# An adaLN block on one core: the first piece of w_mod is issued by ScalarE instead of SyncE

## The chip, the cores and the metric

The kernel runs on one core of one Trainium2 chip. Five engines work side by side, each through its own list of instructions: TensorE (PE: matmuls; PEld: the loading of their stationary operand), VectorE (DVE), ScalarE (ACT), GpSimd (POOL) and SyncE (SP). SP and ACT also issue DMA transfers, each on a queue of its own; the transfers of both queues are carried out by the core's 16 DMA engines. The metric is the time of one execution in microseconds (us).

## The reference

The block takes x, 2048 rows of 640 numbers, and a conditioning vector c of 640.

```
mod = silu(c) @ w_mod          # 640 x 3840: six vectors sa, ca, ga, sb, cb, gb of 640 each
h = layernorm(x) * (1 + ca) + sa
x = x + ga * (attention(h @ wqkv) @ wo)      # 32 heads of 20, causal, window of 256
h = layernorm(x) * (1 + cb) + sb
x = x + gb * ((sigmoid(h @ w_gate) * (h @ w_up)) @ w_down)     # 1536 hidden
```

Everything is stored in bfloat16. What matters here is the first line and the first layernorm: before the first projection with wqkv can run, sa and ca must be known. They come from silu(c) and the first 1280 columns of w_mod.

## The kernel before, in words

The rows of x are worked through in 8 chunks of 256 rows (two blocks of 128). For each chunk the kernel normalises, projects to q, k and v, computes windowed attention, projects with wo, normalises again and runs the MLP. The work of neighbouring chunks is interleaved.

The order is written out by hand. Each operation is registered by `Prog.op` (alias `A`) in the order of the code, and gets its place from the table `PRIO`: the number divided by 5 is its place, and the remainder says which engine runs it, in the order of `ENGS` (0 PE, 1 ACT, 2 DVE, 3 POOL, 4 SP). `schedule` goes through the operations in the order of these numbers, appends each to its engine's list, gives each DMA the next one of 24 semaphores in turn, and gives each tile a buffer. `emit` writes the five lists with their semaphore waits. Within an engine the order is fixed: an instruction whose operand has not come holds all behind it.

The head of the kernel, up to the first projection, is as follows.

- Loads, all through the helper `dma` (its issues carry line 570 in the profile). ACT issues c (1.2 KB, into a corner of the tile oT), then x block 1 (160 KB). SP issues x block 0 (160 KB), then the first 1280 columns of w_mod in five pieces of 128 rows each (`load_bulk` with the tag wm0; 320 KB each, into wd, which is free until the MLP's weights come), then pieces of wqkv with further blocks of x between them. ACT has no other DMA in the head; after its two issues it loads the table for tanh.
- PE first runs matmuls on zeros (line 649, `warm`), three operations of two matmuls each. Then it turns c into a column (line 634), adds a matmul of ones to the accumulator of the modulation, and runs two more operations of `warm`. Then come the five groups of the modulation, one for each piece of w_mod (`fnA`; through line 668, like all matmuls made by `mm`), with a filling matmul on zeros (line 660, `fill`) between them. The ten transposes of the normalised x blocks 0 and 1 stand between the fourth and the fifth group.
- DVE computes the statistics of x block 0 (line 776, two instructions), then c_col, siluc and silubc (the silu of c, repeated 64 times as a matmul operand; lines 636, 638, 640; ACT computes the tanh in it, line 637), then the statistics of x block 1. GpSimd computes the power of minus one half (lines 781 and 783), and DVE normalises both blocks (line 796).
- The transposes are copied out of PSUM into hT (line 839), and once the five groups are through, DVE copies sa and 1 + ca out (mA, line 761). ACT and DVE modulate hT (lines 846 and 847), and the first projection starts (line 668, operands wqkv and hT).

The lines that issue the loads of the head:

```
keep[0], keep[1] = load_x(p_x1, 0, 0), load_x(p_x1, 1, 0, eng="act", tmin=1.25)
load_bulk(wm_ap[0], wm_src[:, :, 0:1280], Rm[0], 0.93, 0.2, "wm0", lat=0.9)
for i in range(4):
    load_w3(320 * i, 320 * i + 320, 1.1, 0.30 + 0.005 * i, "wq" if i < 2 else "wk", lat=0.5)
```

Of the kernel before, what the change touches and what calls it, by code (L numbers as in the profile page):

```python
# [22 lines left out]
SM_SCALE = 1.0 / math.sqrt(DH)  # L23
VW = 22
NDMA = 24
SWITCH = 0.095
ENGATTR = {"pe": "tensor", "act": "scalar", "dve": "vector", "pool": "gpsimd", "sp": "sync"}
ENGS = ("pe", "act", "dve", "pool", "sp")
OVERLAP = {"pe": 0.0, "act": 0.085, "dve": 0.075, "pool": 0.045, "sp": 0.0}


class Res:
# [49 lines left out]
class Prog:  # L82
# [69 lines left out]
    def schedule(self):  # L152


        free = {e: START for e in ENGS}
        bw = 0.0
        lastturn = False
# [4 lines left out]
        pemode = 0  # L162
        portend = 0.0
        freed = {}

        def slot_time(pool, s):
            ten = pool.tenant[s]
            if ten is None:
                if not all(x.done for x in pool.init[s]):
                    return None  # L170
                return max([x.end + x.lat for x in pool.init[s]], default=0.0)
            return None if ten.left else freed[ten]

        def take(t, s):
            ten = t.pool.tenant[s]
            t.prev = list(t.pool.init[s]) if ten is None else list(ten.rel)
            t.slot = s
            t.pool.tenant[s] = t

        for o in sorted(self.ops, key=lambda x: x.prio):  # L180
            assert all(d.done for d in o.deps), o.tag
            e = ENGS[o.prio % 5]
            assert e in o.engs, (o.tag, e)
            o.eng = e
            st = max([o.tmin, free[e] + (SWITCH if e == "pe" and o.mode != pemode else 0.0)]
                     + [d.end + (0.0 if d.eng == "pe" and e == "pe" else d.lat) for d in o.deps])
            if o.isdma and e == "sp":
                st = max(st, bw - QMAX)
            for t in o.tiles:
                if t.slot is None:  # L190
                    step = 1 if t.mate is None else 2
                    best = None
                    for s in range(0, len(t.pool.tenant), step):
                        rts = [slot_time(t.pool, s + k) for k in range(step)]
                        if None not in rts and (best is None or max(rts) < best[0]):
                            best = (max(rts), s)
                    assert best is not None, (o.tag, t.name)
                    if t.mate is None:
                        take(t, best[1])
                    else:  # L200
                        take(t, best[1] + t.odd)
                        take(t.mate, best[1] + 1 - t.odd)
                for x in t.prev:
                    st = max(st, x.end + x.lat)
            if e == "dve" and o.port:
                st = max(st, free["pool"])
            elif e == "pool":
                st = max(st, portend)
            o.start = st
            if e == "pe":  # L210
                pemode = o.mout
            dur = o.dur[e]
            free[e] = st + dur - OVERLAP[e]
            if e == "dve" and o.port:
                portend = free[e]
            if o.isdma:
                turn = o.dlat > 3.0
                if e == "sp" and bw - st > 2.0:
                    free[e] += 0.35 if o.dur[e] > 1.0 else 0.1
                bw = max(st + o.dlat, bw + (MIXED if turn != lastturn and bw > st + o.dlat else 0.0)) + o.work  # L220
                lastturn = turn
                o.end = max(bw - 0.83, st + dur)
                s = rr
                rr = (rr + 1) % NDMA
                dmacnt[s] += 16
                o.key, o.val = f"d{s}", dmacnt[s]
                if dmalast[s] is not None:
                    o.deps.append(dmalast[s])
                dmalast[s] = o
            else:  # L230
                o.end = st + dur
            order[e].append(o)
            o.done = True
            for t in o.tiles:
                t.left -= 1
                if t.left == 0:
                    last = {}
                    for x in t.ops:
                        if x.isdma:
                            last[x] = x  # L240
                    for e2 in ENGS:
                        xs = [x for x in t.ops if x.eng == e2 and not x.isdma]
                        if xs:
                            last[e2] = max(xs, key=lambda x: x.start)
                    t.rel = list(last.values())
                    freed[t] = max(x.end + x.lat for x in t.rel)
        self.order = order
        self.span = max(o.end for o in self.ops)

    def emit(self):  # L250
        nc = self.nc
# [85 lines left out]
def c_pe(n):  # L337
    return max(n, 64) / 2400.0 + 0.0027


PE_EPS = 0.14
PRIO = [
# [117 lines left out]
]  # L460
TR1 = 2
NPH = 3
NPQ = 2
PQ = ()
KEEP = 3
DSAFE = 1.5
START = 0.8
PORTLAG = 0.05
MIXED = 0.55
NPB = 0  # L470
GB = ()
XT0 = 1
# [9 lines left out]
DEDGE = 0.245  # L482
FILL = 1
WSE = (("dve", "pool"), ("dve", "pool"))
QMAX = 4.5
WDT = 72.0
PAIR = 0
PAIRO = 0
# [5 lines left out]
def build(nc, A_x, A_wqkv, A_wo, B_x, B_w_gate, B_w_up, B_w_down, c, w_mod, out, S=2048):  # L494
# [60 lines left out]
    def R(name):  # L555
        return Res(name)
# [8 lines left out]
    def dma(dst, src, work, reads=(), writes=(), prio=50.0, tmin=0.0, tag="dma", extra=(), nonc=False, hold=(), eng="sp", lat=0.08 + DSAFE, dur=0.5, dlat=2.24):  # L565
        def fn(e, _):
            if nonc:
                with nc.allow_non_contiguous_dma(reason="small"):
                    return e.dma_start(dst(), src())
            return e.dma_start(dst(), src())  # L570
        return A(eng, fn, dur, reads=reads, writes=writes, prio=prio, work=work, tmin=tmin, tag=tag, extra=extra, hold=hold, lat=lat, dlat=dlat)
# [23 lines left out]
    def load_x(pool, b, prio, tmin=0.0, eng="sp", extra=()):  # L595
# [6 lines left out]
    wm_src = w_mod.rearrange("(t p) f -> p t f", p=128)  # L602
    Rm = [[R(f"wm{i}_{kt}") for kt in range(NDT)] for i in range(4)]
    wm23 = hhall[:, 0:2 * NDT * D].rearrange("p (t f) -> p t f", t=NDT)
    wm_ap = [wd[:].rearrange("p a b -> p (a b)")[:, 0:6400].rearrange("p (t f) -> p t f", t=NDT),
             wu[:].rearrange("p a b -> p (a b)")[:, 0:6400].rearrange("p (t f) -> p t f", t=NDT),
             wm23[:, :, D:2 * D], wm23[:, :, 0:D]]

    def load_bulk(dst, src, Rs, work, prio, tag, extra=(), cuts=(1, 2, 3, 4, 5), **kw):
        k = 0  # L610
        for m in cuts:
            dma(lambda k=k, m=m: dst[:, k:m, :], lambda k=k, m=m: src[:, k:m, :], work * (m - k), writes=Rs[k:m],
                prio=prio + 0.01 * k, tag=tag, extra=list(extra), **kw)
            k = m
# [37 lines left out]
    for i in range(5):  # L652
        o = A("pe", warm, 0.85 if i < 4 else 0.43, prio=90, reads=[R_z], extra=wprev, tag="warm", writes=[R("w")])
# [302 lines left out]
    last = {"s": fills, "p": []}  # L956
# [350 lines left out]
```

## Time and profile before

| | |
|---|---|
| Time, median of 3 runs | 325.69 us (325.58 to 326.39) |
| Span of the profiled execution, first to last instruction | 324.3 us |
| The profiled execution's own time | given by its span alone; the median of the runs is 1.39 us above it |
| PE busy | 317.3 us, 98% of the span |
| ACT, DVE, POOL busy | 212.3, 211.8, 187.2 us |
| Moved by DMA | 37.85 MB |

Lines of a timeline read: start in us from the first instruction, duration, engine, line, operation, what it writes and reads with shapes, the count of merged instructions, and in brackets the idle time of the engine just before, with what ended it. A q behind an engine's name stands for its sequencer: "ACTq DMA_DIRECT2D" is the issue of a transfer by ScalarE, not the transfer. Lines of waits read: engine, line, who was waited for, total in us, times, longest. Lines of windows read: the stretch, its length, busy time and instructions of PE, PEld, DVE, ACT and POOL, the granted clock, the DMA engines' busy share, and GB/s. Lines of DMA queues read: packets, MB, share of the 16 engines' time; q1 carries what SP issues and q10 what ACT issues. Ends of matmuls are modelled, so a busy PE is not one at its peak, and the granted clock stands at 1.00 in all windows.

### The profile page before, as it was taken

The page shows a single profiled execution, that of the slowest core. Times are in us where ns is not written, and L with a number is a line of the kernel's source. Part 1 is how long each engine was busy: PE and PEld are TensorE (multiplying, and loading weights), DVE is VectorE, ACT ScalarE, POOL GpSimd, SP SyncE. Part 2 cuts the span into 40 slices and gives each one's busy share as a digit, 9 for nine tenths or more (in the row PEclk, how much of TensorE's full clock was granted, in tenths as well). Part 3 has the DMA queues.
Part 4 walks back from the last instruction along what each step waited for, and adds up shares of the span by engine and source line. Part 5 has one row for each costly group of instructions (what it writes and reads, how often), then busy time and mean ns, then how long its engine had stood idle before and what let it go on. Part 6 is the DMA issues. An engine that isn't in the chain of part 4 may idle for free.

```text
span 324.3 us, 11594 instructions
## 1 busy us (share of the span) xinstructions
PE 317.3 (98%) x4872; PEld 222.7 (69%) x4873; DVE 211.8 (65%) x424; ACT 212.3 (65%) x316; POOL 187.2 (58%) x276
## 2 busy tenths in 40 slices
PE   8999999989999999999999999999999999999997
PEld 3564545446776568765776467877786788787885
DVE  5797898778687959674477475837463769264332
ACT  1899985889876687788687867786767764011120
POOL 5128869976668694847585939382939691012100
DMA  7998799989891383824405394340213032202101
GB/s 249 371 333 299 165 269 180 200 137 183 260 164 22 83 109 77 152 61 101 85 22 82 97 103 110 92 69 5 81 40 88 3 79 53 76 20 64 40 2 40
DMA packets 71694, 37.85 MB, mean 117 GB/s; under 512 B 45274, under 2 KB 70362, under 8 KB 71642
## 3 DMA queue, kind: packets, MB, share of 16 engines
q1 hardware_dynamic: 69616, 35.31, 48.3%
q10 hardware_dynamic: 2026, 1.80, 2.1%
q8 instruction: 38, 0.62, 0.8%
q14 instruction: 14, 0.11, 0.1%
HBM read 21.30 MB, written 5.25 MB: 82 GB/s over the span
## 4 chain that ended last, share of the span: by engine, by line
PE 73%; DMA 2%; SPq 2%; DVE 1%; POOL 1%; issue 0%; DVEq 0%
PE M L668 61%; PE S L669 6%; PE M L669 5%; DMA gbc<-gate 2%; SPq L803 2%; DVE wd L1192 1%; POOL x L793 0%; POOL st L788 0%; DVE hh L1211 0%; POOL E L1040 0%; DVE x L1230 0%; DVEq L310 0%
## 5 line engine op out<-in xcount | busy, mean ns | idle before, releaser
L1040 POOL TENSOR_SCALAR_AFFINE_SELECT E<-E 128x512 bf16<-128x512 bf16 (+1 forms) x176 | 142.6, 836 | 68.7 <-ACT E L1015 67.0
L1015 ACT ACTIVATE E<-S 128x512 bf16<-128x512 f32 (+2 forms) x184 | 150.9, 878 | 47.4 <-PE S L669 46.5
L668 PE MATMUL M<-wqkv,hT 128*128 128x480 bf16 (+1 forms) x340 | 73.9, 355 | 0.6 <-ACT hT L846 0.5
L668 PE MATMUL M<-h2T,wu 128*128 128x256 bf16 x480 | 68.0, 273 | 0.5 <-DVE hh L1211 0.5
L668 PE MATMUL M<-h2T,wg 128*128 128x256 bf16 x480 | 67.8, 273 | 0.0
L668 PE MATMUL M<-wd,hh 128*128 128x320 bf16 (+2 forms) x396 | 58.1, 295 | 0.0
L1209 ACT ACTIVATE sig<-M 128x512 f32<-128x512 f32 x48 | 28.9, 602 | 44.1 <-PE M L668 41.7
L1211 DVE SCALAR_TENSOR_TENSOR hh<-sig,M 128x512 bf16<-128x512 f32 x48 | 32.4, 681 | 37.1 <-ACT sig L1209 24.0
L668 PEld LDWEIGHTS M<-h2T,wu 128*128 128x128 bf16 x480 | 45.9, 98 | 8.4 <-issue 1.2
L668 PEld LDWEIGHTS M<-h2T,wg 128*128 128x128 bf16 x480 | 45.7, 98 | 7.1
L668 PEld LDWEIGHTS M<-wqkv,hT 128*128 128x128 bf16 x340 | 30.1, 98 | 27.6 <-DMA wqkv<-in_A_wqkv_dram 1.6
L668 PEld LDWEIGHTS M<-wd,hh 128*128 128x128 bf16 x396 | 36.8, 98 | 14.3 <-DVE hh L1211 0.2
L669 PEld LDWEIGHTS S<-QT,KT 20*64 20x64 bf16 (+1 forms) x1856 | 19.9, 100 | 21.3 <-ACT E L1015 12.0
L1230 DVE TENSOR_TENSOR x<-M,x 128x320 bf16<-128x320 f32 (+2 forms) x33 | 15.6, 476 | 27.2 <-PE M L668 27.2
L669 PE MATMUL S<-QT,KT 20*64 20x256 bf16 (+5 forms) x1856 | 32.1, 228 | 1.2 <-ACT E L1015 1.2
L776 DVE BATCH_NORM_STATS2 st<-x 128x6 f32<-128x320 bf16 x64 | 28.6, 477 | 2.3 <-DMA x<-in_A_x_dram 1.9
L1082 DVE STREAM_TRANSPOSE T<-M 128x512 f32<-128x512 f32 x32 | 21.5, 698 | 9.2 <-PE S L669 8.0
L668 PE MATMUL M<-wo,oT 128*128 128x320 bf16 x160 | 25.4, 299 | 0.0
L669 PE MATMUL M<-E,V 128*32 128x128 bf16 (+1 forms) x960 | 22.8, 246 | 0.8 <-ACT E L1015 0.4
L781 POOL TENSOR_SCALAR st<-st 128x2 f32<-128x2 f32 x16 | 3.7, 234 | 33.8 <-DVE st L778 33.6
L669 PEld LDWEIGHTS M<-E,V 128*32 128x32 bf16 x960 | 19.2, 97 | 5.3 <-issue 2.9
L1091 DVE STREAM_TRANSPOSE On<-Tn 128x1024 bf16<-128x1024 bf16 x16 | 19.8, 1240 | 0.3
(77 smaller groups left out, 240.2 us busy)
## 6 DMA issues: line engine op xcount, KB each, us to landing
x<-in_A_x_dram SPq DMA_DIRECT2D x23, 160.0 KB, 2.3
doc<-On SPq DMA_DIRECT2D x56, 40.0 KB
wd<-in_B_w_down_dram SPq DMA_DIRECT2D x4, 480.0 KB
wd<-in_w_mod_dram SPq DMA_DIRECT2D x5, 320.0 KB
wqkv<-in_A_wqkv_dram SPq DMA_DIRECT2D x4, 400.0 KB
wu<-in_w_mod_dram SPq DMA_DIRECT2D x5, 320.0 KB
oT<-doc SPq DMA_DIRECT2D x8, 192.0 KB, 2.5
out_dram<-x SPq DMA_DIRECT2D x9, 160.0 KB
```

Source lines behind the costliest of these rows:

```text
L668: return e.matmul(o, l, r, start=st, stop=sp, skip_group_check=True)
L669: return e.matmul(o, l, r, start=st, stop=sp, tile_position=tp, skip_group_check=True)
L776: A("dve", lambda e, g, bi=bi, j=j: e.bn_stats(v(bi * 12 + j * 6, 6), src[bi].ap[:, j * 320:(j + 1) * 320]), 0.48, reads=[src[bi].r()], wr ...
L781: A("pool", lambda e, g: e.tensor_scalar(v(28, n), var(), EPS, None, op0=ALU.add), 0.2, reads=[st.r(("m", bi)) for bi in range(n)], writes ...
L803: return e.dma_start_transpose(dst(), src())
L1015: A("act", lambda e, eng: e.activation(dst(), src(), ACT.Exp, scale=SM_SCALE), c_act(n), reads=[Sp.r()], writes=[E.r(key)], prio=3, tag=f" ...
L1040: A("pool", lambda e, eng: e.affine_select(rows(dst), rows(src), pattern=[[0, 8], [sign, n]], compare_op=ALU.is_ge, fill=0.0, base=base, c ...
L1082: A("dve", lambda e, g, h=h: e.transpose(T1.ap[:, 512 * h:512 * h + 512], X[h].ap), 0.694, reads=[X[h].r()], writes=[T1.r(h)], prio=3.5, t ...
L1091: A("dve", lambda e, g: e.transpose(On.ap[:], Tn.ap[:]), 1.22, reads=[Tn.r()], writes=[On.r()], prio=4, tag=f"tr2_{a}")
L1209: A("act", lambda e, g, pg=pg, sg=sg: e.activation(sg.ap[:], pg.ap[:], ACT.Tanh, scale=0.5), c_act(512), reads=[pg.r()], writes=[sg.r()], ...
L1211: A("dve", lambda e, g, pu=pu, sg=sg, f0=f0: e.scalar_tensor_tensor(out=hh.ap[:, f0:f0 + 2, :], in0=sg.ap[:].rearrange("p (a b) -> p a b", ...
L1230: A("dve", lambda e, g, ps=ps, bi=bi, c0=c0, n=n: e.tensor_tensor(x1[bi].ap[:, c0:c0 + n], ps.ap[:, 0:n], x1[bi].ap[:, c0:c0 + n], op=ALU. ...
```

## The change

The load of the first w_mod piece may now be issued by ACT or SP, and the table gives it to ACT, at place 15, where c stood. c (76 to 81), x block 0 (84 to 89) and two statistics instructions of DVE (87 to 92 and 92 to 97) move back by one place each, which changes nothing on SP and DVE: x block 0 is still SP's first issue, and the other four pieces follow it. ACT's list now begins with the first piece of w_mod, c, x block 1.

The rest of the diff takes the planner's estimate of times out of `schedule`. It had chosen each tile's buffer by these estimates; the choices are now written out in the table `SLOTS`, one number for each of 709 tiles, and they are the buffers that the estimate chose before. The first four DMA semaphores are dealt out in the new order.

```diff
 PRIO = [
-    23, 28, 258, 8, 43, 33, 958, 18, 1448, 38, 3, 507, 513, 72, 67, 48, 53, 58, 76, 84, 101, 99, 144, 149, 154, 159,
+    23, 28, 258, 8, 43, 33, 958, 18, 1448, 38, 3, 507, 513, 72, 67, 48, 53, 58, 81, 89, 101, 76, 144, 149, 154, 159,
...
-    92, 87, 187, 237, 242, 247, 253, 263, 272, 267, 280, 275, 290, 300, 305, 286, 317, 296, 322, 311, 376, 357, 386,
+    97, 92, 187, 237, 242, 247, 253, 263, 272, 267, 280, 275, 290, 300, 305, 286, 317, 296, 322, 311, 376, 357, 386,
...
             for t in o.tiles:
                 if t.slot is None:
...
+                    s = SLOTS[tiles[t]] if SLOTS else 0
+                    ten = t.pool.tenant[s]
...
-    load_bulk(wm_ap[0], wm_src[:, :, 0:1280], Rm[0], 0.93, 0.2, "wm0", lat=0.9)
+    load_bulk(wm_ap[0], wm_src[:, :, 0:1280], Rm[0], 0.93, 0.2, "wm0", lat=0.9, eng=("act", "sp"))
```

More of the change, by code (lines that the diff above doesn't have):

```diff
@@ L161, in schedule, with number @@
         rr = 0
[L162 to L178, printed above, removed]
+        tiles = {}
+        def number(t):
+            if t is not None and t not in tiles:
+                tiles[t] = len(tiles)
+                number(t.mate)
+        for o in self.ops:
+            for t in o.tiles:
+                number(t)
         for o in sorted(self.ops, key=lambda x: x.prio):
@@ L184, in schedule @@
             o.eng = e
[L185 to L188, printed above, removed]
             for t in o.tiles:
                 if t.slot is None:
[L191 to L215, printed above, removed]
-            if o.isdma:
[L217 to L223, printed above, removed]
-                rr = (rr + 1) % NDMA
[L225 to L231, printed above, removed]
+                    s = SLOTS[tiles[t]] if SLOTS else 0
@@ new lines, in schedule @@
+                    ten = t.pool.tenant[s]
+                    assert ten is not None or all(x.done for x in t.pool.init[s]), (o.tag, t.name)
+                    assert ten is None or ten.left == 0, (o.tag, t.name)
+                    t.prev = list(t.pool.init[s]) if ten is None else list(ten.rel)
+                    t.slot = s
+                    t.pool.tenant[s] = t
+            if o.isdma:
+                dmacnt[rr] += 16
+                o.key, o.val = f"d{rr}", dmacnt[rr]
+                if dmalast[rr] is not None:
+                    o.deps.append(dmalast[rr])
+                dmalast[rr] = o
+                rr = (rr + 1) % NDMA
@@ L237, in schedule @@
                     last = {}
[L238 to L244, printed above, removed]
+                    for x in sorted(t.ops, key=lambda x: x.prio):
+                        last[x if x.isdma else x.eng] = x
                     t.rel = list(last.values())
-                    freed[t] = max(x.end + x.lat for x in t.rel)
         self.order = order
-        self.span = max(o.end for o in self.ops)
     def emit(self):
@@ L460 @@
 ]
+SLOTS = [
[20 rows of a table added]
+]
 TR1 = 2
@@ L466 @@
 DSAFE = 1.5
-START = 0.8
-PORTLAG = 0.05
-MIXED = 0.55
 NPB = 0
```

7 lines of the change are left out of this document (removed), and 20 rows, old and new, of the table SLOTS.

## The prediction, made before the result was known

> **What bounds the kernel now.** I read four views in this order: the page, the whole-run waits of TensorE, the timelines of the first 16 us, and the DMA rates of that stretch. The page first:
>
> ```profile
> span 324.3 us, 11594 instructions
> ...
> PE 317.3 (98%) x4872; PEld 222.7 (69%) x4873; DVE 211.8 (65%) x424; ACT 212.3 (65%) x316; POOL 187.2 (58%) x276
> ...
> PE 73%; DMA 2%; SPq 2%; DVE 1%; POOL 1%; issue 0%; DVEq 0%
> ```
>
> TensorE is busy for 317.3 of 324.3 us, so what is left to gain or lose is the idle time of PE, and any stretch in which PE runs late. Of TensorE's waits over the whole run, these bear on the sum:
>
> ```profile
> PE S L669 <- ACT E L1015: 1.2, 4, 0.4
> PE M L668 <- DVE hh L1211: 0.5, 1, 0.5
> PE M L668 <- ACT hT L846: 0.5, 1, 0.5
> ```
>
> The first two lie in the attention and in the first MLP. The third is the end of the head: the first projection waits for the modulated hT. Because PE has almost no idle time behind it, a head that ends later pushes nearly everything behind it by the same amount. So the change is priced at the first projection. How PE gets there (PE's timeline):
>
> ```profile
> 3.98 0.18 PE L634 MATMUL M<-ident,oT 5*128 5x5 bf16 x1
> ...
> 6.04 0.58 PE L668 MATMUL S<-silubc,wd 128*128 128x64 bf16 x10
> ...
> 8.11 0.47 PE L668 MATMUL S<-silubc,wd 128*128 128x64 bf16 x10 [0.19 <-DMA wd<-in_w_mod_dram]
> 8.44 0.62 PE L668 MATMUL M<-ident,x 128*128 128x128 bf16 x8
> ...
> 10.36 2.33 PE L668 MATMUL M<-wqkv,hT 128*128 128x320 bf16 x15 [0.47 <-ACT hT L846]
> ```
>
> At 3.98 PE turns the conditioning vector c (it lands in oT), right behind the warm-up matmuls. From 6.04 it multiplies the five w_mod pieces (wd), at 8.44 it transposes the normalised x blocks 0 and 1, and at 10.36 projects. VectorE's timeline of the same time:
>
> ```profile
> 3.08 0.89 DVE L776 BATCH_NORM_STATS2 st<-x 128x6 f32<-128x320 bf16 x2 [1.42 <-DMA x<-in_A_x_dram]
> 4.20 0.17 DVE L636 TENSOR_SCALAR c_col<-M 128x5 bf16<-128x5 f32 x1 [0.23 <-PE M L634]
> ...
> 4.84 0.49 DVE L640 COPY silubc<-siluc 128x320 bf16<-128x320 bf16 x1
> 5.24 0.88 DVE L776 BATCH_NORM_STATS2 st<-x 128x6 f32<-128x320 bf16 x2
> ...
> 7.58 0.80 DVE L796 TENSOR_SCALAR x<-x,st 128x640 bf16<-128x640 bf16 x2 [1.22 <-POOL st L783]
> ...
> 9.50 0.17 DVE L761 COPY mA<-S 128x10 f32<-128x10 f32 x1
> ```
>
> This is the chain that sets the head: c_col, the copy silubc, then with no gap the statistics of x block 1 (5.24 to 6.12), the power on GpSimd, the normalisation until 8.38, and PE's transposes 0.06 us later, at 8.44. It starts from PE's 3.98. That instant is set by the warm-up in front of it, and the change does not touch it. The modulation mA follows at 9.50, behind the transposes and PE's last w_mod group.
>
> **The change part by part.** It moves one 320 KB load, the first w_mod piece, from SP's list, second place, to ACT's list, first place. The issues as they stand (timelines of ScalarE and SyncE):
>
> ```profile
> 0.79 0.57 ACTq L570 DMA_DIRECT2D oT<-in_c_dram  x1
> 1.40 0.37 ACTq L570 DMA_DIRECT2D x<-in_A_x_dram  x1
> 1.80 1.28 ACT L637 ACT_TABLE_LOAD   x1 [1.80 <-issue]
> 4.40 0.21 ACT L637 ACTIVATE cth<-c_col 128x5 f32<-128x5 bf16 x1 [1.32 <-DVE c_col L636]
> ```
> ```profile
> 0.79 0.39 SPq L570 DMA_DIRECT2D x<-in_A_x_dram  x1
> 1.25 2.31 SPq L570 DMA_DIRECT2D wd<-in_w_mod_dram  x5
> ```
>
> One w_mod issue costs 2.31 / 5 = 0.46 us of its queue. (1) On SP the four other pieces and everything behind them go out up to 0.46 us earlier. (2) The moved piece goes out at 0.79 instead of 1.25, also 0.46 earlier. (3) On ACT, c goes from 0.79 to 1.25, x block 1 from 1.40 to 1.86, the table load from 1.80 to 2.26, ending 3.54. The tanh that needs the table runs at 4.40, so the table load costs nothing: 0.86 us of idle time hide it, and past that ACT would delay silubc one for one. No wait is added and no other instruction moves.
>
> What the earlier pieces are worth: the windows of 0.5 and 1 us (last two columns: DMA share, GB/s) and the loads of weights by TensorE.
>
> ```profile
> 2.50:3.00 0.50, 0.50 (x3) 0.16 (x2) 0.00 (x0) 0.50 (x1) 0.50 (x7) 1.00 0.98 218
> 3.00:3.50 0.50, 0.50 (x3) 0.14 (x1) 0.42 (x2) 0.08 (x1) 0.50 (x3) 1.00 0.67 248
> ...
> 4.00:5.00 1.00, 1.00 (x5) 0.51 (x5) 0.60 (x4) 0.21 (x1) 0.45 (x1) 1.00 1.01 357
> ```
> ```profile
> 7.23 0.35 PEld L668 LDWEIGHTS S<-silubc,wd 128*128 128x128 bf16 x10 [0.20 <-DMA wd<-in_w_mod_dram]
> ...
> 8.10 0.35 PEld L668 LDWEIGHTS S<-silubc,wd 128*128 128x128 bf16 x10 [0.49 <-DMA wd<-in_w_mod_dram]
> ...
> 13.28 0.54 PEld L668 LDWEIGHTS M<-wqkv,hT 128*128 128x128 bf16 x5 [0.18 <-DMA wqkv<-in_A_wqkv_dram]
> ...
> 14.76 0.52 PEld L668 LDWEIGHTS M<-wqkv,hT 128*128 128x128 bf16 x5 [0.31 <-DMA wqkv<-in_A_wqkv_dram]
> ```
>
> Between 2.5 and 3.5 us the engines moved a mean of 233 GB/s, against 357 behind it. That hole is (357 - 233) / 357 x 1 us = 0.35 us of transfer. Filling it brings the whole stream of w_mod and wqkv forward by at most 0.35 us; the lower bound is nothing (the hole only moves). What PE can take of it is less. Its waits for w_mod at 7.23 and 8.10 are followed by transposes that the VectorE chain holds anyway (8.38 against 8.44), so I count nothing there. The two waits for wqkv, 0.18 + 0.31 = 0.49 us, can shrink; PE's own timeline shows no idle time of note there, as earlier matmuls still run beside a weight load, so between 0 and 0.49, and I take 0.2, nearer the 0.31 less that overlap. Where the head ends late, these waits shrink too, since PE comes later to the same data.
>
> What the later loads cost. The ACT queue's packets (q10), in 1.50 to 2.75, 2.75 to 3.50 and 3.50 to 4.75 us:
>
> ```profile
> q10 hardware_dynamic: 10, 0.00, 0.6%
> ...
> q10 hardware_dynamic: 8, 0.01, 3.7%
> ...
> q10 hardware_dynamic: 136, 0.15, 36.9%
> ```
>
> The first 10 packets are c, the other 144 are x block 1, mostly after 3.5. Three arrivals come under pressure.
> - c: data done by 2.75, used at 3.98, so up to 1.2 us of cover. It loses 0.46 by its place and more by standing behind 320 KB in the same queue. Shared evenly with SP's queue that piece takes 2 x 320 KB / 357 GB/s = 1.8 us. From a start of data between 1.5 and 2, where c's own packets are now, that is 3.3 to 3.8, and c would just make 3.98: I take 0; the high end, c held longer, is a rival below.
> - x block 0: it now shares the engines with the moved piece from the start. Alone it landed by 3.08; behind a whole piece it would come 320 / 357 = 0.9 us later. VectorE's idle 0.23 us ahead of c_col covers part: between 0 and 0.67 late, at a fair share about 0.3.
> - x block 1: its statistics start at 5.24 without a wait; its data ended by 4.75, so its slack is between 0 and 0.49. Low end: the slack covers the 0.46, cost 0. High end: 0.46 and a whole piece more, which by the distance of the two w_mod waits (8.10 - 7.23) is 0.87: together 1.33. A gain is excluded, since the statistics stand behind silubc. I take 0.5, the issue shift with next to no slack, because its packets come so late (136 of 144 after 3.5).
>
> All three enter the same VectorE chain, so the largest counts and not their total: the first projection comes 0.5 late. **Sum:** +0.5 for the head, -0.2 for the wqkv waits, = +0.3 us. The span goes from 324.3 to 324.6; the median of the runs, 325.69, is 1.39 above this profile's span, and I add the 0.3 to it: 326.0. Since 0.3% is 0.98 us, about what a measurement of this kernel can tell from no change, this is no change that could be told.
>
> The Trainium skill's page DMA: Bandwidth & Descriptors (Queues, rings and completion order) says that each DMA engine alternates between the queues packet by packet, and takes the descriptors of one queue in order; by that, c and x block 1 do stand behind the moved piece. The same page (Issuing engines are not separate DMA queues) says that issuing from several engines saves only issue time: by that the gain could not pass 0.46 us, where the hole in the rows gives 0.35.
>
> **The rivals.** *A whole piece in front (slower).* c or x block 1 is held until the moved piece is through, at ACT's queue. For it: before, x block 1 was issued at 1.40 and most of its packets came after 3.50, so that queue was served late even with little ahead of it. Against it: c, in front of it, had its data by 2.75. Price: 1.33 - 0.2 = +1.1, that is 326.8. It decides once the chain is over 1.18 us late, the statistics of x block 1 starting after 6.4.
>
> *TensorE's clock rises later (slower).* If c is late, PE stands still at 3.98, in the midst of its warm-up. The groups of PE by form, of the same 512 columns:
>
> ```profile
> L649 PE MATMUL S<-E 128*128 128x512 bf16 x10 | 4.7, 631 | 1.3 <-DVE E L644 1.3
> ...
> L660 PE MATMUL S<-E 128*128 128x512 bf16 x4 | 1.5, 380 | 0.1
> ```
>
> The warm-up ones take 0.25 us more than the fills that run from 6.46 on. Were PE still at the slow pace from 6.04 to 9.5, its 50 x 64, 10 x 128 and 4 x 512 columns (12.75 times 512) would cost up to 3.2 us more, at least 0; small matmuls are bound by their issue and the waits for w_mod cover some, so about half, 1.6: 327.3. Against it: PE stays busy from 1.31 on unless c passes 3.98. The Trainium skill's TensorE: Matmul & The Clock Gate (Part 1) has the clock rise after a busy window of some 3.4 us; one more window at half speed would be an estimate of 1.7 us lost.
>
> *The earlier stream counts in full (a little faster).* x block 1 keeps its slack, and the wqkv waits shrink by 0.35: 325.3. For it: the hole. Against it: the VectorE chain at 8.38. To be faster by over 0.98, PE's waits for E and hh (1.2 + 0.5) would have to go too, by a shift against the DMA further on; nothing in the profile ties them to it.
>
> *Nothing arrives earlier or later:* the transfers are bound by the engines and the order of 480 KB in front is not felt, 325.7.
>
> **How the numbers follow.** My forecast, +0.3: 0.41. No effect: 0.06. A little faster: 0.10. A whole piece in front: 0.23. The late clock: 0.12. Faster by over 0.98: 0.08. The first three make 0.57, of which 0.02, the forecast's upper tail, lies over the bound: 0.55 within 0.3%. The two slow rivals and that tail make 0.37 slower, and 0.08 is left for faster. The predicted time is the likeliest case's, 326.0, whose own range is 325.7 to 326.6. For 8 in 10 the range goes from 325.1, below the little gain, to 327.5, which takes in the whole piece and the late clock's middle.
>
> **What would show it.** Right: ScalarE issues wd first and c at about 1.25; SP's wqkv issues start near 3.1; the rate in 2.5 to 3.5 us is near 350; x block 1's statistics start near 5.7 with a wait for DMA; PE's first projection is near 10.9 and its wqkv waits are shorter. Wrong: c_col well after 4.2 with PE idle at 3.98 (c was not covered), fills that still take 0.6 us (the clock), or a first projection before 10.36.

## The result and the profile after

The changed kernel takes 327.98 us, the median of 7 runs (326.97 to 330.79), against 325.58 us (325.22 to 326.39, 7 runs) for the kernel before on the same chip. The ratio is 1.0082, with a 95% interval of 1.0061 to 1.0103: slower by 2.4 us. The prediction was 326.0 us with a range of 325.1 to 327.5; the time lies above it. The runs of the changed kernel also spread more: in three of the seven the mean granted clock is 0.99 or 0.995, and these three are the slowest (328.75 to 330.79); the other four took 326.97 to 327.98, with a median of 327.25. The profile is of the run that took 327.03.

In the changed kernel line numbers are 34 lower (the 668 of before is 634, 776 is 742, 570 is 536). The page's first lines of the profiled execution:

```profile
span 325.3 us, 11594 instructions
...
PE 316.9 (97%) x4872; PEld 223.0 (69%) x4873; DVE 211.4 (65%) x424; ACT 212.1 (65%) x316; POOL 186.7 (57%) x276
```

The work is the same to the instruction, and PE is busy for no longer than before (316.9 against 317.3 us). What was added is idle time of PE. The waits of TensorE over the whole run:

```profile
PE M L634 <- DVE x L762: 1.6, 1, 1.6
```

Two waits are new: this one, 1.6 us for the normalised x, ahead of the transposes, and 0.5 us for c, which stands in TensorE's timeline below. The issues went out as the diff says (ScalarE's and SyncE's timelines, start and duration first):

```profile
0.80 0.41 ACTq L536 DMA_DIRECT2D wd<-in_w_mod_dram  x1
1.24 0.58 ACTq L536 DMA_DIRECT2D oT<-in_c_dram  x1
1.85 0.36 ACTq L536 DMA_DIRECT2D x<-in_A_x_dram  x1
```
```profile
1.25 1.92 SPq L536 DMA_DIRECT2D wd<-in_w_mod_dram  x4
3.22 1.02 SPq L536 DMA_DIRECT2D wqkv<-in_A_wqkv_dram  x2
```

c and x block 1 are issued 0.45 us later than before. What that does to the head stands on VectorE's and TensorE's timelines:

```profile
4.44 0.89 DVE L742 BATCH_NORM_STATS2 st<-x 128x6 f32<-128x320 bf16 x2 [2.78 <-DMA x<-in_A_x_dram]
5.25 0.15 DVE L602 TENSOR_SCALAR c_col<-M 128x5 bf16<-128x5 f32 x1
...
7.14 0.89 DVE L742 BATCH_NORM_STATS2 st<-x 128x6 f32<-128x320 bf16 x2 [0.78 <-DMA x<-in_A_x_dram]
```
```profile
4.50 0.18 PE L600 MATMUL M<-ident,oT 5*128 5x5 bf16 x1 [0.45 <-DMA oT<-in_c_dram]
...
10.34 0.62 PE L634 MATMUL M<-ident,x 128*128 128x128 bf16 x8 [1.64 <-DVE x L762]
...
12.27 2.28 PE L634 MATMUL M<-wqkv,hT 128*128 128x320 bf16 x15 [0.47 <-ACT hT L812]
```

All three loads are late. Block 0's statistics start at 4.44 (before 3.08), PE's turn of c at 4.50 (3.98), and block 1's statistics at 7.14 (5.24), now behind a wait for DMA. c_col, at 5.25 (4.20), waits for nothing but the end of block 0's statistics: by PE's turn of c, behind which it came by 0.22 us before, it could have run at 4.72. From there on the chain is that of before: the transposes come at 10.34 (8.44) and the first projection at 12.27 (10.36), 1.91 us later. The chain of waits up to 13 us names the transfer:

```profile
1.85 5.27 DMA x<-in_A_x_dram
```

Issued at 1.85, x block 1 landed 5.27 us later, at 7.12. Before, it was issued at 1.40 and was there by 5.24 at the latest, when its statistics began without a wait. So 0.45 us of later issue became at least 1.88 us of later arrival: that is what the experiments had to explain.

The traces also record when each of the 16 parts of a load is reported as landed; no view prints it. The issue of each load and its list, and from these records the landing of its last part, in us:

| Load | Before: issued, landed | After: issued, landed |
|---|---|---|
| x block 0, 160 KB | 0.79 SP, 3.06 | 0.79 SP, 4.42 |
| w_mod piece 1, 320 KB | 1.25 SP, 4.95 | 0.80 ACT, 4.65 |
| x block 1, 160 KB | 1.40 ACT, 5.11 | 1.85 ACT, 7.12 |
| w_mod piece 2 | 1.71 SP, 6.35 | 1.25 SP, 5.45 |
| w_mod piece 3 | 2.17 SP, 7.19 | 1.71 SP, 6.92 |
| w_mod piece 4 | 2.65 SP, 8.06 | 2.18 SP, 7.72 |

In both kernels these loads land in the order in which they were issued, whichever list issued them. x block 1 has moved from third place to fifth, and from 5.11 to 7.12: 2.01 us.

Further on, three places on TensorE's timeline, before and then after:

```profile
15.55 0.40 PE L669 MATMUL S<-QT,KT 20*128 20x256 bf16 x8
...
84.78 1.26 PE L668 MATMUL M<-h2T,wg 128*128 128x256 bf16 x10
86.54 1.25 PE L668 MATMUL M<-h2T,wu 128*128 128x256 bf16 x10 [0.51 <-DVE hh L1211]
```
```profile
17.25 0.40 PE L635 MATMUL S<-QT,KT 20*128 20x256 bf16 x8
...
86.42 1.25 PE L634 MATMUL M<-h2T,wg 128*128 128x256 bf16 x10
87.51 1.25 PE L634 MATMUL M<-h2T,wu 128*128 128x256 bf16 x10
```

PE is 1.91 us late at the first projection and 1.70 at the first scores (17.25 against 15.55): 0.2 is given back at the wqkv waits. It is still 1.64 late at 86.42. Then before waits 0.51 us for hh and after doesn't, and 0.97 is left (87.51 against 86.54), which stays to the end: the spans of the two profiled runs differ by 1.0 us, the medians of the times by 2.4. The wait for hh need not be there in every run of before: the profile of the last experiment below has the same head as before, no such wait, and a span of 323.7 us instead of 324.3.

### The profile page after: what moved, and what is told of

The parts are those of the page before. It is cut to its first block, busy times and chain, and to the rows that moved or that the text cites. A ratio compares the mean times of both kernels' runs of the same rounds, so it can differ in the third digit from the quotient of the medians.

```text
span 325.3 us, 11594 instructions
## 1 busy us (share of the span) xinstructions
PE 316.9 (97%) x4872; PEld 223.0 (69%) x4873; DVE 211.4 (65%) x424; ACT 212.1 (65%) x316; POOL 186.7 (57%) x276
## 3 DMA queue, kind: packets, MB, share of 16 engines
HBM read 21.30 MB, written 5.25 MB: 82 GB/s over the span
## 4 chain that ended last, share of the span: by engine, by line
PE 92%; ACT 3%; DMA 2%; issue 1%; DVE 1%; ACTq 1%; POOL 0%
PE M L634 76%; PE S L635 8%; PE M L635 7%; ACT E L981 2%; DMA x<-in_A_x_dram 2%; ACTq L536 1%; ACT hT L777 0%; DVE st L742 0%; ACT hT L805 0%; DVE x L762 0%; POOL st L749 0%; DVE hT L824 0%; ACT hT L812 0%; DVE x L1196 0%; POOL st L747 0%
```

## The experiments

Three theories stood against each other ("theory C" in the first expectation is that the late c alone counts). Order (O): transfers issued by SP and by ACT are served in the order of their issue, over both queues. Then x block 1, which had 480 KB issued ahead of it (x block 0 and one w_mod piece), now has 1120 KB (x block 0 and three pieces, issued at 0.80, 1.25 and 1.71). Queue (Q): as the prediction's slow rival had it, only the piece ahead in ScalarE's own queue counts. Clock (K): the loss is TensorE's, whose clock falls or rises late because PE stands still. All edits are to the table of places, unless told. In it the first row holds, among others, the places of c, x block 0, x block 1 and the first w_mod piece; the remainder by 5 is the engine (1 ACT, 4 SP); the diffs show these four numbers alone. No experiment leaves out work.

**c first on ScalarE** (from the changed kernel: c, w_mod piece, x block 1):

```diff
-    81, 89, 101, 76,
+    76, 89, 101, 81,
```

> ScalarE issues c, then the w_mod piece, then x block 1. Theory O (transfers of both queues are served in the order of issue, as in one line): ahead of x block 1 there are still x block 0 and three w_mod pieces, 1120 KB as in the changed kernel, so its statistics start near 7.1 and the first projection near 12.2; c is back to its old place, so TensorE's 0.45 us wait for c is gone, and nothing is won by that: span near 325.3, time 326.5 to 328. Theory C (the late c is what counts): the first projection comes back to 11.3 or earlier and the time to about 326.

Measured: 327.62 us (327.16 to 329.0, 6 runs), ratio to before 1.0068 (1.0047 to 1.0089). VectorE's and TensorE's timelines, and the windows (the number ahead of the last two columns is the granted clock):

```profile
7.75 0.89 DVE L742 BATCH_NORM_STATS2 st<-x 128x6 f32<-128x320 bf16 x2 [2.43 <-DMA x<-in_A_x_dram]
```
```profile
3.98 0.18 PE L600 MATMUL M<-ident,oT 5*128 5x5 bf16 x1
...
10.96 0.62 PE L634 MATMUL M<-ident,x 128*128 128x128 bf16 x8 [2.07 <-DVE x L762]
...
12.88 1.49 PE L634 MATMUL M<-wqkv,hT 128*128 128x320 bf16 x5 [0.33 <-ACT hT L812]
```
```profile
12.00:13.00 1.00, 0.63 (x2) 0.14 (x2) 0.96 (x6) 1.00 (x4) 0.00 (x0) 0.57 1.11 365
13.00:14.00 1.00, 1.00 (x5) 0.49 (x4) 1.00 (x5) 0.94 (x3) 0.00 (x0) 0.50 1.10 380
14.00:15.00 1.00, 1.00 (x6) 0.52 (x5) 0.97 (x4) 0.44 (x1) 0.00 (x0) 0.50 1.08 372
15.00:16.00 1.00, 1.00 (x7) 0.65 (x6) 0.97 (x5) 0.26 (x1) 0.22 (x1) 0.72 1.08 364
```

c is in time again (PE at 3.98, without a wait) and nothing is won: x block 1, issued at 1.79, alone holds the head. Here PE's clock can be seen to fall: after 2.07 us of idle PE the granted clock falls to 0.50 between 12 and 13 us and is back in the window from 15 to 16. Two of the six runs show such a fall in their mean clock (0.995), the profiled one (328.87 us) among them; they are the slowest.

**x block 1 second on ScalarE** (c, x block 1, w_mod piece):

```diff
-    81, 89, 101, 76,
+    76, 89, 81, 101,
```

> ScalarE issues c, x block 1, then the w_mod piece; SyncE as in the changed kernel. Theory O: only x block 0 and one piece go ahead of x block 1, 480 KB as in the kernel before, so its statistics start at 5.2 to 5.4; the first w_mod piece now stands behind 960 KB and the first w_mod group on TensorE starts at 6.2 to 6.6; first projection 10.4 to 10.6, time 325.5 to 326.0. Theory Q (only what stands ahead in the same queue delays, the queues alternating packet by packet): the same for x block 1, the first w_mod group on time at 6.04.

Measured: 328.03 us (326.59 to 329.25, 6 runs), ratio 1.0074 (1.0051 to 1.0096). VectorE's and TensorE's timelines:

```profile
5.25 0.88 DVE L742 BATCH_NORM_STATS2 st<-x 128x6 f32<-128x320 bf16 x2
```
```profile
8.09 0.47 PE L634 MATMUL S<-silubc,wd 128*128 128x64 bf16 x10 [1.84 <-DMA wd<-in_w_mod_dram]
```

x block 1, issued at 1.42, is in time (5.25, no wait). Now the w_mod piece, issued last at 1.81, is late: PE waits 1.84 us for it. Issued by ScalarE at 1.8, 160 KB and 320 KB are late alike. Both theories had expected the first group earlier, O at 6.2 to 6.6 and Q at 6.04, and O the time at 325.5 to 326.0. The order itself was kept: SP's piece issued at 1.70 landed at 7.87, ScalarE's at 8.04. Of each, nine of the 16 parts were there by 6.7; the last parts came late. The profile is of the quickest run. In four of the six the mean clock is 0.994 or 0.995, so the median holds more than the late head.

**x block 1 on SyncE, behind x block 0** (ScalarE: w_mod piece, c):

```diff
-    81, 89, 101, 76,
+    81, 89, 94, 76,
-    keep[0], keep[1] = load_x(p_x1, 0, 0), load_x(p_x1, 1, 0, eng="act", tmin=1.25)
+    keep[0], keep[1] = load_x(p_x1, 0, 0), load_x(p_x1, 1, 0, eng=("act", "sp"), tmin=1.25)
```

> The changed kernel with x block 1 issued by SyncE, right behind x block 0; ScalarE issues the w_mod piece and c. Theory O (transfers of both queues land in the order of issue): ahead of x block 1 are x block 0 and the moved piece, 480 KB as in the kernel before, so it lands by about 5.1 and no longer sets the head; what is left is that x block 0 shares the engines with the moved piece and c stands behind it, so c_col starts near 5.2 as in the changed kernel, against 4.2, and the head is about 1.0 us late in place of 1.9: first projection 11.2 to 11.5, time 326.4 to 327.0. If x block 1 is the only thing that is late, the first projection is at 10.4 and the time 325.7.

Measured: 326.58 us (326.06 to 327.44, 10 runs), ratio 1.0032 (1.002 to 1.0045). VectorE's timeline, then TensorE's:

```profile
4.26 0.89 DVE L742 BATCH_NORM_STATS2 st<-x 128x6 f32<-128x320 bf16 x2 [2.60 <-DMA x<-in_A_x_dram]
5.06 0.15 DVE L602 TENSOR_SCALAR c_col<-M 128x5 bf16<-128x5 f32 x1
...
6.09 0.88 DVE L742 BATCH_NORM_STATS2 st<-x 128x6 f32<-128x320 bf16 x2
```
```profile
4.69 0.18 PE L600 MATMUL M<-ident,oT 5*128 5x5 bf16 x1 [0.65 <-DMA oT<-in_c_dram]
...
8.27 0.61 PE L626 MATMUL S<-E 128*128 128x512 bf16 x1
...
9.23 0.39 PE L626 MATMUL S<-E 128*128 128x512 bf16 x1
...
9.75 0.61 PE L634 MATMUL M<-ident,x 128*128 128x128 bf16 x8
...
11.66 2.28 PE L634 MATMUL M<-wqkv,hT 128*128 128x320 bf16 x15 [0.47 <-ACT hT L812]
```

With x block 1 in time, more than half of the 2.4 us is gone: the head is 0.6 us earlier than in the changed kernel (11.66 against 12.27), and no run shows a fall of the clock. What is left is x block 0 and c. Block 0's statistics start at 4.26 (3.08 before), c_col follows them without a gap at 5.06 (4.20), and so block 1's statistics start 0.85 us late and the normalisation too (8.43 against 7.58). c comes 0.65 us late; c_col does not feel that, but PE stands still in its warm-up, and the filling matmul still takes 0.61 us at 8.27 (0.38 in the kernel before from 6.46 on). PE reaches the transposes at 9.75 without a wait, 1.31 us later than before and some 0.5 us after the normalised x was ready (8.43 + 0.80 = 9.23). That is the prediction's clock rival, by its mechanism, but it adds 0.5 us of head and not its price of 1.6. The granted clock stands at 1.00 in the windows of this stretch all the same; only the durations show the slow pace.

**The kernel before with a tiny load in front of c** (1.2 KB, c once more, into a spare tile):

```diff
+    c_two = sb("c_two", [NDT, 128])
+    dma(lambda: c_two[:], lambda: c.rearrange("o (t p) -> (o t) p", p=128), 0.05, writes=[R("ctwo")], eng="act", lat=0.3, at=71)
```

> The kernel before, with a second load of c (1.2 KB) into a spare tile as ScalarE's first issue: c and x block 1 are issued about 0.6 us later, with nothing large ahead of them on ScalarE's queue, and no w_mod piece moved. Theory O: x block 1, issued near 2.0, now comes after SyncE's second w_mod piece (issued at 1.71), 320 KB or 0.87 us more ahead of it: its statistics start at 6.0 to 6.4, the first projection at 11.1 to 11.5, time 326.4 to 327.0. Theory Q (only what stands ahead in the same queue delays): at most the 0.6 us of issue less its slack, statistics at or before 5.7, first projection 10.4 to 10.8, time 325.7 to 326.1.

> The kernel with the tiny extra load in front of c, looked at a second time. Order of issue alone (x block 1 issued 0.3 to 0.45 us later, so behind one more w_mod piece): the statistics of x block 1 start at 5.6 to 6.4, the first projection at 10.7 to 11.6. If a later place on ACT's queue costs more than the order of issue: again near 7.9 and 13. If the 7.95 of the first look was one slow packet, this look shows another start than 7.9.

> As the look before it: 5.6 to 6.4 by the order of issue alone, near 7.9 if the place on the queue costs more, and differing from look to look if single slow packets decide.

Measured: 327.17 us (326.67 to 328.92, 6 runs), ratio 1.0056 (1.0037 to 1.0075); the two later runs, one of each, took 326.83 and 326.80. x block 1 is issued at 1.69 or 1.70, by 0.3 us later than before. VectorE's timelines of the three profiles:

```profile
7.95 0.89 DVE L778 BATCH_NORM_STATS2 st<-x 128x6 f32<-128x320 bf16 x2 [2.63 <-DMA x<-in_A_x_dram]
```
```profile
6.71 0.89 DVE L778 BATCH_NORM_STATS2 st<-x 128x6 f32<-128x320 bf16 x2 [1.38 <-DMA x<-in_A_x_dram]
```
```profile
6.93 0.89 DVE L778 BATCH_NORM_STATS2 st<-x 128x6 f32<-128x320 bf16 x2 [1.61 <-DMA x<-in_A_x_dram]
```

Here no w_mod piece stands in ScalarE's queue at all. 2.4 KB are ahead of x block 1 there, and still its statistics start 1.5 to 2.7 us late, for 0.3 us of later issue. So Q isn't the cause. But the order alone doesn't give all of it either: it puts x block 1 level with the piece that SP issues at 1.71, which makes 5.6 to 6.4. Most of the load did come so early: nine of its 16 parts had landed by 5.29, 5.29 and 5.45 in the three profiles, the last at 7.92, 6.69 and 6.91, each time just ahead of that piece (8.09, 6.87, 7.12). What changes from profile to profile is the last parts. In the trace single packets took 0.8 to 1.7 us there, against some 0.1 for most, which fits late last parts. Why they do is open.

c itself does not keep the order here: issued at 1.39, after SP's first piece (1.24 or 1.25), it landed at 3.0 to 3.4, and that piece at 4.2 to 4.3. So a load of 1.2 KB can pass a large one of the other list.

**x block 1 on SyncE in the kernel before** (ScalarE issues c alone, SyncE all five w_mod pieces behind both x blocks):

```diff
-    76, 84, 101, 99,
+    76, 84, 89, 99,
```

> The kernel before with x block 1 issued by SyncE, right behind x block 0 and ahead of all w_mod pieces; ScalarE issues c alone. If the head of the kernel before is held by the chain from c_col and by the w_mod pieces, an earlier x block 1 wins nothing: statistics still at 5.2, first projection 10.2 to 10.5, time 325.4 to 326.0. If x block 1 is itself late in the kernel before, the first projection comes before 10.2 and the time is below 325.3.

Measured: 326.34 us (325.65 to 327.0, 8 runs), ratio 1.0023 (1.0012 to 1.0035). TensorE's timeline:

```profile
6.36 0.47 PE L668 MATMUL S<-silubc,wd 128*128 128x64 bf16 x10 [0.62 <-DMA wd<-in_w_mod_dram]
...
11.18 1.99 PE L668 MATMUL M<-wqkv,hT 128*128 128x320 bf16 x12 [0.47 <-ACT hT L846]
```

x block 1 in front wins nothing (its statistics stay at 5.23, behind silubc on VectorE), and the pieces, all issued 0.45 us later, cost PE waits for w_mod and the head 0.8 us. So before was tight on both sides.

**x block 1, w_mod piece, c on ScalarE** (from the changed kernel):

```diff
-    81, 89, 101, 76,
+    86, 89, 76, 81,
```

> The changed kernel with ScalarE's order x block 1, w_mod piece, c. Theory O: ahead of c (1.2 KB, issued near 1.65) are both x blocks and two w_mod pieces, 960 KB, so c lands at 5.0 to 5.6 and TensorE, its warm-up done at 3.9, waits 1.1 to 1.7 us for it; the first projection is at 11.5 to 12.1, time 327 to 328. Theory Q: ahead of c are only the 480 KB of its own queue: it lands at 4.3 to 4.8 and the first projection is at 10.8 to 11.3.

Measured: 327.64 us (327.41 to 328.12, 4 runs), ratio 1.0064 (1.0051 to 1.0077). The chain of waits, TensorE's timeline and a window:

```profile
1.71 4.39 DMA oT<-in_c_dram
```
```profile
6.14 0.17 PE L600 MATMUL M<-ident,oT 5*128 5x5 bf16 x1 [2.10 <-DMA oT<-in_c_dram]
```
```profile
8.00:9.00 1.00, 1.00 (x16) 0.72 (x14) 0.48 (x2) 0.00 (x0) 0.31 (x3) 0.50 1.13 358
```

c is 1.2 KB. Issued at 1.71 behind both x blocks and two to three w_mod pieces (960 to 1280 KB over both queues, 480 KB in its own), it lands 4.39 us later, at 6.10, half a microsecond behind the piece ahead of it in its own queue (5.60) and ahead of SP's piece issued at 1.70 (6.79). Both theories had it earlier, O at 5.0 to 5.6 and Q at 4.3 to 4.8. For c, the load in its own queue explains the wait as well as the order does; the runs do not part the two. PE stands still for 2.10 us, and the granted clock falls here too, to 0.50; in three of the four runs the mean clock is 0.995.

**Fills in the idle time of PE** (the changed kernel with 8 more matmuls on zeros ahead of the transposes), and **PE held up in the kernel before** (9 of them ahead of its transposes, all loads as before):

```diff
+    fills.append(fill(8, oA[3:4], oA[3].prio + 0.5))
```

> The changed kernel with eight more matmuls on zeros in the stretch in which TensorE waits for x (8.5 to 10.3 us); nothing else differs, and the head ends as late as in it, first projection near 12.3. Theory K (part of the loss is TensorE's clock falling after that idle stretch, in some runs): the granted clock is 1.000 in every run, the times lie within 0.5 us of each other near 327, at least 0.7 under the changed kernel's median of 327.98. If the clock has nothing to do with it: the same median and the same spread, 327 to 331.

> The kernel before, all loads as they were, with nine matmuls on zeros between the fourth w_mod group and the transposes, which holds the head back by 1.9 us with TensorE busy; first projection near 12.3. If a late head is the whole loss of the fast span, the span is 325.2 to 325.6 and the time 326.5 to 327.0, granted clock 1.000 in all runs: of 1.9 us about 0.9 is given back later. If the later transfers by themselves cost something beyond the head, this kernel is faster than that, under 326.2.

Measured: the filled one 327.74 us (326.93 to 328.48, 6 runs), ratio 1.0061 (1.0044 to 1.0077), and the held one 327.77 us (327.1 to 329.1, 6 runs), ratio 1.0069 (1.0049 to 1.0088). The mean clock is 1.0 in all twelve runs. The first projection of the second:

```profile
12.85 1.33 PE L668 MATMUL M<-wqkv,hT 128*128 128x320 bf16 x8 [0.47 <-ACT hT L847]
```

In the filled kernel the falls of the clock are gone, and with them the slowest runs (none above 328.48, where the changed kernel had 328.75 to 330.79). The median loses only 0.24 us, so K is an addition and not the main cause; that is less than the 0.7 that had been expected of it. Over all kernels the falls go with long stops of PE: a mean clock of 0.995 or less stands in 13 of the 29 runs of the five kernels whose profile shows a stop of 1.5 us or more (the changed kernel, c first, x block 1 second, the tiny load, x block 1 first), and in none of the 42 runs of the five other variants that were run several times.

The second kernel prices a late head with all loads issued as before: 2.49 us at the first projection of its profile (12.85 - 10.36) go with 2.10 us of time (327.77 - 325.67). Of the 2.49, the matmuls on zeros make 1.9; the fourth w_mod group had come 0.59 late in this run (8.70 against 8.11). About 0.4 is given back on the way, not the larger part.

**The changed kernel, once more.** 

> The changed kernel, looked at a second time. Order of issue: x block 1 (issued at 1.85 behind x block 0 and three w_mod pieces) lands again after 6.9, its statistics wait until 7.0 to 7.8, the first projection starts at 12.2 to 12.9. If the first look was an accident of slow packets: the statistics before 6.5.

Measured: 326.60 us. VectorE's and TensorE's timelines, and the w_mod groups of 4 to 9.2 us by form (busy time, mean ns), of this profile and then of the first:

```profile
6.70 0.89 DVE L742 BATCH_NORM_STATS2 st<-x 128x6 f32<-128x320 bf16 x2 [0.57 <-DMA x<-in_A_x_dram]
```
```profile
4.63 0.18 PE L600 MATMUL M<-ident,oT 5*128 5x5 bf16 x1 [0.58 <-DMA oT<-in_c_dram]
...
9.90 0.62 PE L634 MATMUL M<-ident,x 128*128 128x128 bf16 x8
...
11.82 2.28 PE L634 MATMUL M<-wqkv,hT 128*128 128x320 bf16 x15 [0.47 <-ACT hT L812]
```
```profile
L634 PE MATMUL S<-silubc,wd 128*128 128x64 bf16 x30 | 2.2, 244 | 0.0
```
```profile
L634 PE MATMUL S<-silubc,wd 128*128 128x64 bf16 x40 | 2.0, 200 | 0.0
```

The statistics of x block 1 wait again, until 6.70; it landed at 6.68, again after the piece issued at 1.71 (6.29). That is earlier than the 7.0 to 7.8 expected by the order, and later than the 6.5 below which the first profile would have been an accident. In this profile c is 0.58 us late (0.45 in the first), and PE stays at the slow pace: 244 ns a matmul against 200. It arrives at the transposes about when the normalised x does. So two delays lie beside each other here, each worth over 1 us of the head, and to take one away leaves the other.

**The piece on ScalarE behind c, x block 1 on SyncE behind x block 0**:

```diff
-    81, 89, 101, 76,
+    76, 89, 94, 81,
-    keep[0], keep[1] = load_x(p_x1, 0, 0), load_x(p_x1, 1, 0, eng="act", tmin=1.25)
+    keep[0], keep[1] = load_x(p_x1, 0, 0), load_x(p_x1, 1, 0, eng=("act", "sp"), tmin=1.25)
```

> The piece of w_mod stays on ACT's queue, but c is issued in front of it (at 0.79), and x block 1 goes out on SP behind x block 0 (near 1.25), so that the order of issue is that of the kernel before, but for the piece and x block 1, which change places within 0.2 us. If only the order of issue counts: c at PE in time (PE's turn of c at 3.98 without a wait), the statistics of x block 1 start without a wait near 5.25, PE at the fast pace from 6.05, the first projection at 10.3 to 10.7, and the time within 0.3% of the kernel before, 325.4 to 326.4. If a w_mod piece on ACT's queue costs by itself (by the place it takes beside SP's, or by ACT's later table load), the first projection comes after 11 and the time is above 326.6.

Measured: 325.93 us (325.13 to 327.59, 12 runs) against 325.60 (17 runs), ratio 1.0011 (0.9997 to 1.0025): no difference that can be told. VectorE's and TensorE's timelines:

```profile
5.24 0.88 DVE L742 BATCH_NORM_STATS2 st<-x 128x6 f32<-128x320 bf16 x2
```
```profile
3.98 0.18 PE L600 MATMUL M<-ident,oT 5*128 5x5 bf16 x1
...
10.36 2.35 PE L634 MATMUL M<-wqkv,hT 128*128 128x320 bf16 x15 [0.47 <-ACT hT L812]
```

The piece still goes out on ScalarE, at 1.41, and the queues of piece and x block 1 are exchanged against before. But the order of issue is that of before, save that these two change places, and the head is back to the hundredth: 5.24, 3.98, 10.36. Beside the kernel with c first (12.88 and 327.62) x block 1 goes out at 1.25 on SP instead of 1.79 on ACT, and SP's four pieces 0.46 us later, behind it. That change of place is worth 2.5 us of head. For the two loads that were exchanged the queue counts for nothing; when they go out, for nearly all.

The landings say the same of all fourteen profiles: the loads of 160 KB and more that go out in the first 4 us land in the order of their issue over both lists, but for two pieces in one kernel that were issued 0.01 us apart.

## Why the prediction was wrong

*The issues, the table load and the chain* were right: c and x block 1 go out 0.45 us later, SP's wqkv at 3.22, and the head is set by the statistics of x block 1, as foreseen.

*x block 1, taken as 0.5 late with a high end of 1.33, was 1.90 late* (5.24 to 7.14; 1.46 in the second profile). This is the step that failed. It counted the later issue and, at most, one piece more, the one in ScalarE's own queue. But SP's pieces count as well: one more of them (issued at 1.71) went out ahead of x block 1, so that 1120 KB instead of 480 KB stood in front, two pieces more and not one. At the prediction's own 357 GB/s, 640 KB take 1.8 us; the landing moved by 2.01 us in the first profile (5.11 to 7.12) and by 1.57 in the second (6.68). The prediction had the row that points there, 136 of 144 packets after 3.50 with next to nothing ahead in that queue, and used it for a rival at 0.23 instead of for the price. Its slack, taken as next to none, was 0.13 (5.24 - 5.11): that part was right. What settles it are the landings of the large loads, in the order of issue in every profile, the tiny load (not the own queue) and the last experiment (order restored, loss gone). The order does not give the whole size: the tiny load cost more than the bytes ahead explain, by last parts that came late.

With 1.90 in place of 0.5 the prediction's sum is 1.9 - 0.2 = 1.7, or 327.4, and the four runs without a fall of the clock have a median of 327.25. The rest of the 2.4 us goes with the three runs in which the clock fell, a term that the prediction had at nothing for a stop of PE at this place. The split is rough: the filled kernel, without such falls, still took 327.74.

*x block 0, taken as 0.3 late with at most 0.67, was 1.36 late* (3.08 to 4.44). Issued at the same moment as the moved piece, it came later than even a whole piece ahead (0.9 by the prediction's rate) would have made it. It moved c_col by 1.05 (4.20 to 5.25), all of it by itself, as c would have let it run at 4.72. It was then hidden behind x block 1, and came out in the run with x block 1 on SyncE, where it set 0.85 us of the head. So this term was too small as well, by a factor of three, and its high end too low.

*c, taken at nothing* ("would just make 3.98"), came 0.45 to 0.65 late in four profiles. Its sum of 3.3 to 3.8 shared the piece with SP's queue evenly, from a start that was too early: the piece landed at 4.65 and c at 4.46. With x block 1 in time, block 0 and c together cost about 0.9 us of time (326.58 against 325.72), and c's part, through the slow pace of PE, is some 0.5 of the 1.3 us of head. In the changed kernel both are covered by x block 1, as the run with c first shows.

*The wqkv waits, -0.2,* were right: 1.91 becomes 1.70, and TensorE's weight loads no longer wait for wqkv. *The hole in the stream* was filled where it was said, but opened earlier. The windows (last two columns: DMA share, GB/s) of the changed kernel:

```profile
2.00:2.50 0.50, 0.50 (x2) 0.15 (x1) 0.00 (x0) 0.26 (x1) 0.50 (x3) 1.00 0.69 110
...
3.00:3.50 0.50, 0.50 (x3) 0.14 (x1) 0.00 (x0) 0.50 (x1) 0.50 (x2) 1.00 0.95 358
```

From 3.0 to 3.5 us 358 GB/s are moved instead of 248, and from 2.0 to 2.5 only 110 instead of 252. The first wqkv load landed 0.26 us earlier (9.70 against 9.96).

*A late head pushes what is behind it by the same amount:* nearly, 2.10 of 2.49 in the held-up kernel.

*The rivals.* "A whole piece in front" had the right transfer and the right sign, and its own condition came true (the statistics after 6.4). Its 326.8 was too low because it put one piece in front and not two, and because it had no fall of the clock. "TensorE's clock rises later" is real in the run with x block 1 on SyncE, at 0.5 us of head; in the changed kernel's second profile it lies beside the other loss, and in the first it did not happen. What it had not was the second place: PE idle before the transposes, after which the clock falls in some runs, which made the three slowest ones.

The rule of the Trainium skill that was weighed (DMA: Bandwidth & Descriptors, Queues, rings and completion order), that an engine alternates between its queues packet by packet, would let x block 1 in the changed kernel, with one piece and c ahead of it in its queue, go ahead of SP's third load, if it is read load by load. It landed after that load (7.12 against 6.92, and 6.68 against 6.29 in the second profile), and the measurement decides. The statement of the Trainium skill's same page that issuing from several engines saves only issue time (Issuing engines are not separate DMA queues) agrees with the gain, which was no more than that; it was the place ahead of the other list's loads that cost some 2 us.

The Trainium skill's page TensorE: Matmul & The Clock Gate (Part 1) has the clock go by windows of some 3.4 us that run free of the kernel. The profiles agree in kind: PE was at the fast pace from about 6.9 in the first profile of the changed kernel, and from about 9.2 in the run with x block 1 on SyncE, and the fall in the run with c first lasted about that long (0.57, 0.50, 0.50 and 0.72 in the windows from 12 to 16 us, that is 0.43 + 0.50 + 0.50 + 0.28 = 1.71 us lost, at half speed 3.4 us). The Trainium skill has the clock fall there after an idle window, 3.4 us; here it followed idle stretches of 2.07 and 2.10 us, and the measurement decides.

## What to carry to other kernels

Where SP and ACT both issue loads, count the bytes that go out ahead of a large load on either list, by the time of issue, and price its delay by the bytes that newly get in front of it: here half a microsecond of issue time was two 320 KB pieces and some 2 us. Ask it of every load that moves: x block 0, which shared its instant of issue with a piece, was 1.36 us late. Put the smallest loads that something waits for first, and don't start a large one in the same instant. And look at what a late load does to PE: besides its idle time, a stop of half a microsecond in the warm-up or of two behind it can cost a second loss through the clock, which only shows when the first is repaired.

## What had not been expected

- A load of 1.2 KB can wait as long as a large one: 4.39 us from issue to landing for c, behind 480 KB in its own queue. With only 1.2 KB ahead of it in its own queue it passed a 320 KB piece of the other list (1.39 to 3.0 or 3.4).
- The slow pace of PE in the warm-up isn't in the granted clock, which shows 1.00 while the filling matmul takes 0.61 us in place of 0.38; the fall after an idle stretch is (0.50).
- A stop of PE of 0.58 and 0.65 us in the warm-up went with a fast pace that came only at 9.2 us; stops of 0.45 and 0.51 us went with 6.9 and 5.5. Without a stop it came between 5.1 and 7.1 in eight profiles, by the distances of single matmuls. What decides was not tried.
- The same tiny extra load made x block 1's statistics start at 6.71, 6.93 and 7.95 in three profiles.
